# Rebuilding the opening of a gated-recurrence and two-way-maximum kernel: fp32 token halves, weights in three groups, block 0 and block 1 interleaved

## The chip, the cores and the metric

The kernel runs on one core of a Trainium2 chip, as a single launch. The metric is the device time in microseconds, the median of several runs. The engines are TensorE (PE, its weight loads listed as PEld), VectorE (DVE), ScalarE (ACT), GpSimd (POOL) and SyncE (SP), which only issues transfers.

## The reference

The inputs are `x` and `f_logit` (4 x 6144 x 256), `lower_bound` (256), and three matrices `w1`, `w2` (256 x 1024) and `w_out` (1024 x 256), all in float32.

```python
sig = 1 / (1 + exp(-f_logit))
f = lower_bound + (1 - lower_bound) * sig
for t in range(S):                       # h starts at 0 for each of the 4 sequences
    h = f[:, t] * h + (1 - f[:, t]) * x[:, t]
    y[:, t] = h
out = maximum(y @ w1, y @ w2) @ w_out    # on the 24576 rows of y
```

## The kernel before, in words

**Algebra.** With u = sigmoid(-f_logit) the input gate is (1 - lower_bound) * u, and the decay is 1 - (1 - lower_bound) * u. The kernel's recurrence is driven by v = u * x, so its y is smaller than the reference's by the factor `om` = 1 - lower_bound for each channel; the weights are multiplied by `om` instead. `nom` = lower_bound - 1 makes the decay out of u. The maximum is written as y @ w1 + relu(y @ (w2 - w1)), so the kernel needs `wd` = om * (w2 - w1) for its first layer, `w_out` as it is (`wob`, in bfloat16), and `w13` = om * (w1 @ w_out) for the part that passes by the relu.

**Tiles.** The 24576 tokens are 48 blocks of 512. Channels lie on the partitions (two halves of 128, `h` or `kc`), tokens along the free axis. The 1024 hidden units are eight groups of 128 (`fc`). The blocks are fetched in chunks: chunks 0 to 3 are one block each, the later ones two. For chunks 1 to 3, POOL's queue casts the tokens to bfloat16 on the way into SBUF (`fn`, `xn`) and PE turns them (`turn_steps`, `turn`, tiles `tT` in a PSUM pool of two). For the later chunks POOL's queue writes a bfloat16 copy to scratch memory (`scr`), and SP's queue brings it back transposed (`cross`, tiles `fT`, `xT`).

**One block.** `gate` is a sigmoid on ACT (u). `scan_steps` is a list of DVE steps: two decays (`ff`), one product over both halves (`v`), two scans (`y`). `first_layer(j, fc)` is two 512-column matmuls into a PSUM tile `dT` (pool of three) and a relu on ACT into `rt`. `second_layer` is, for each 128 tokens, two 256-column matmuls of y with `w13` and eight of `rt` with `wob`, into `psO` (pool of three); DVE copies two of them at a time to `osb`, and SP stores the block.

**Order.** The order of work on each engine is written out by hand (`tc.manual_schedule()`); only the semaphores and the slots of the pools are assigned by the framework. In the steady loop, iteration j has, for each fc, the first layer of block j, an eighth of the second layer of block j - 1, and one step of block j + 1's recurrence.

**The opening.** SP's queue fetches `lower_bound`, then block 0 as two halves of 256 tokens for each of `f_logit` and `x` (`fetch_first`, tiles `raw`, fp32), then w2 and w1 in two groups of four fc. POOL waits for the first group of w2 (`pool_waits`), then issues `w_out`, chunks 1 to 3 and the first scratch copies. Block 0's halves are cast to bfloat16 (`first_bf16`; DVE for the first half, ACT for the second), turned on PE (`first_turn`) and run through `first_recurrence` (sigmoid on ACT, decays, product and scans on DVE). `make_wd` subtracts in fp32 on DVE and scales, on ACT for group 0 and on DVE for group 1. w1 is turned on PE (`turn_w1`), copied by DVE (`keep_w1T`), and `make_w13` multiplies it with `wob`. After that block 1 is turned, and block 0's second layer follows as a whole:

```python
make_w13()
turn(turn_steps(1))
recurrence(1)
ahead("cross", cross, 4)
for fc in range(FC):
    second_layer(0, fc)
turn(turn_steps(2))
gate(2)
for fc in range(FC):
    first_layer(1, fc)
for step in scan_steps(2):
    step()
```

Then block 3 is turned and gated, and iteration j = 2 does the whole second layer of block 1 with block 3's recurrence beside it, and then the first layer of block 2.

Of the kernel before, what the change touches and what calls it, by code (L numbers as in the profile page):

```python
# [18 lines left out]
def kernel(  # L19
# [95 lines left out]
    raws = {}  # L115

    def fetch_first(k):
        nt = TB // 2
        for s in range(2):
            raw = const.tile([P, nt // P, D], FP32, name=f"raw{k}{s}")  # L120
            nc.sync.dma_start(  # L121
                out=raw[:],
                in_=srcs[s][0, k * nt : (k + 1) * nt, :].rearrange(
                    "(p i) d -> p i d", p=P
                ),
            )
            raws[k, s] = raw

    def first_bf16(k, s, copy):
        raw = raws[k, s]  # L130
        nat = const.tile([P, raw.shape[1], D], BF16, name=f"nat{k}{s}")
        copy(out=nat[:], in_=raw[:])  # L132
        raws[k, s] = nat

    def first_turn(k):
        nt = TB // 2
        for s in range(2):
            dst = ps_t.tile([P, KC, nt // P, P], BF16, name="tT")
            for q in range(nt // P):
                for h in range(KC):  # L140
                    nc.tensor.transpose(  # L141
                        dst[:, h, q, :],
                        raws[k, s][:, q, h * P : (h + 1) * P],
                        ident[:],
                    )
            raws[k, s] = dst[:].rearrange("p k i m -> p k m i")
# [48 lines left out]
    def like(t, src):  # L195
        if len(src.shape) == 3:
            return t
        return t.rearrange("p k (m i) -> p k m i", m=P)

    def scan_steps(j):  # L200
# [17 lines left out]
        def drive():  # L218
            xT = turned[j, 1]
            nc.vector.tensor_tensor(  # L220
                out=like(v[:, :, 0:nb], xT),
                in0=like(u[:, :, 0:nb], xT),
                in1=xT,
                op=ALU.mult,
            )

        def scan(h):
# [15 lines left out]
            lambda: decay(0),  # L243
            lambda: decay(1),
            drive,
            lambda: scan(0),
# [5 lines left out]
    def first_recurrence(k):  # L252
        nt = TB // 2
        cols = slice(k * nt, (k + 1) * nt)
# [4 lines left out]
        u, ff, v, y = (*(first[t] for t in ("u", "ff", "v")), ys[0])  # L259
        fT, xT = raws[k, 0], raws[k, 1]  # L260
# [3 lines left out]
        for h in range(KC):  # L264
            nc.vector.tensor_scalar(
                out=ff[:, h, cols],
                in0=u[:, h, cols],
                scalar1=nom[:, h : h + 1],
                scalar2=1.0,
                op0=ALU.mult,  # L270
                op1=ALU.add,
            )
        nc.vector.tensor_tensor(
            out=like(v[:, :, cols], xT), in0=like(u[:, :, cols], xT), in1=xT,
            op=ALU.mult,
        )
        for h in range(KC):
            nc.vector.tensor_tensor_scan(
                out=y[:, h, cols],
                data0=ff[:, h, cols],  # L280
                data1=v[:, h, cols],
                initial=y[:, h, nt - 1 : nt] if k else 0.0,
                op0=ALU.mult,
                op1=ALU.add,
            )

    def recurrence(j):
        gate(j)
        for step in scan_steps(j):
            step()  # L290
# [6 lines left out]
    lbc = const.tile([P, KC], FP32)  # L297
    waited = const.tile([P, 1], FP32)
    warm = const.tile([P, 1], FP32)
    wob = wpool.tile([P, FC, D], BF16)  # L300
    wdf = wpool.tile([P, KC, DFF], FP32)
# [3 lines left out]
    NG = 2  # L305
    NQ = FC // NG
# [140 lines left out]
    with tc.manual_schedule():  # L447
# [8 lines left out]
        for g in range(NG):  # L456
            fetch_w(g)
# [114 lines left out]
```

## Time and profile before

| | before |
|---|---|
| Median of 9 runs | 400.65 us (400.54 to 438.31) |
| The profiled execution, device time | 400.69 us |
| The profiled execution, span | 398.9 us |
| PE busy | 388.5 us in 2792 matmuls |
| DVE busy | 249.0 us |
| ACT busy | 269.5 us |
| POOL busy | 26.4 us |

The span is the stretch from the first to the last instruction of the program; the device time contains some 1.8 us around it. Busy time does not contain waits. A matmul row has a modelled end, and matmuls overlap, so the distance from one start to the next is what counts on PE. In a row of the timeline the first number is the start in microseconds from the beginning of the span, the second the length of the row, and "x8" the number of instructions merged in it; in a row of the groups, the numbers after the bar are the busy time in microseconds, the mean of one in nanoseconds, and the idle time in front with what ended it.

### The profile page before, as it was taken

Reading aid. Unit: us, or ns where it says so; the run is one execution under the profiler, and the core shown is the slowest. Engines: PE = TensorE matmul, PEld = TensorE weight load, DVE = VectorE, ACT = ScalarE, POOL = GpSimd, SP = SyncE. Lnnn points to the kernel's source line nnn. Section 1 sums busy time; section 2 is a strip of 40 time slices with the busy share of each in tenths; the row PEclk is TensorE's granted clock in tenths of the full one; section 3 lists DMA queues with packets and bytes.
Section 4 is the critical chain, followed back from the end, with each engine's and each line's share of the span. In section 5 each row is a group of like instructions: output and inputs, shape, how many; then the busy total and the mean of one; then the engine's idle time right before and its main releaser. Section 6 shows DMA issues by size and latency. Waiting matters only on the chain.

```text
span 398.9 us, 7018 instructions
## 1 busy us (share of the span) xinstructions
PE 388.5 (97%) x2792; PEld 294.9 (74%) x2792; DVE 249.0 (62%) x359; ACT 269.5 (68%) x447; POOL 26.4 (7%) x58
## 2 busy tenths in 40 slices
PE   3999999999999999999999999999999999999996
PEld 2677777777777777777777777777777777777775
DVE  5886666567656756665676567566656765665641
ACT  3656766776676667667766766776676667667761
POOL 2400010000000000000000000000000000000000
PEclk9999999999999999999999999999999999999999
DMA  7999999898998999699699999998996996762212
GB/s 244 243 244 197 160 187 285 143 250 195 194 245 193 220 219 214 183 240 193 178 180 236 209 170 247 175 211 219 195 220 176 237 209 166 165 128 89 101 53 108
DMA packets 103377, 77.01 MB, mean 193 GB/s; under 512 B 93552, under 2 KB 94064, under 8 KB 102640
## 3 DMA queue, kind: packets, MB, share of 16 engines
q1 hardware_dynamic: 100512, 51.13, 53.8%
q0 software_dynamic: 2544, 25.17, 37.3%
q8 instruction: 22, 0.36, 0.4%
q10 hardware_dynamic: 288, 0.26, 0.2%
q14 instruction: 11, 0.09, 0.1%
HBM read 53.48 MB, written 48.23 MB: 255 GB/s over the span
## 4 chain that ended last, share of the span: by engine, by line
PE 97%; DMA 2%; SPq 1%; issue 0%; DVE 0%
PE psO L410 53%; PE dT L381 42%; DMA w1n<-in_moe_w_dram 2%; PE psO L352 1%; PE tT L180 1%; PE psO L365 0%; SPq L121 0%; SPq L448 0%; SPq L321 0%; DVE osb L419 0%
## 5 line engine op out<-in xcount | busy, mean ns | idle before, releaser
L389 ACT ACTIVATE rt<-dT 128x512 bf16<-128x512 f32 x384 | 222.0, 598 | 109.6 <-PE dT L381 109.6
L410 PE MATMUL psO<-wob,rt 128*128 128x256 bf16 x1536 | 228.5, 273 | 0.0
L381 PE MATMUL dT<-y,wd 128*128 128x512 bf16 x768 | 227.3, 382 | 0.0
L410 PEld LDWEIGHTS <-rt 128*128 128x128 bf16 x1536 | 169.9, 113 | 39.9
L430 DVE COPY osb<-psO 128x512 f32<-128x512 f32 x94 | 64.9, 691 | 71.9 <-PE psO L410 71.9
L233 DVE TENSOR_TENSOR_SCAN y<-ff,y,v 128x512 bf16<-128x512 bf16 x88 | 107.9, 1267 | 0.1
L381 PEld LDWEIGHTS <-wd 128*128 128x128 bf16 x768 | 75.2, 98 | 11.0 <-issue 2.1
L410 PE MATMUL psO<-w,y 128*128 128x256 bf16 x384 | 73.3, 273 | 0.0
L410 PEld LDWEIGHTS <-y 128*128 128x128 bf16 x384 | 43.1, 113 | 39.9
L209 DVE TENSOR_SCALAR ff<-u,nom 128x512 bf16<-128x512 bf16 x94 | 28.9, 350 | 66.7 <-ACT u L190 66.7
L190 ACT ACTIVATE u<-fT 128x1024 bf16<-128x1024 bf16 x44 | 46.2, 1049 | 0.0
L220 DVE TENSOR_TENSOR v<-u,xT 128x1024 bf16<-128x1024 bf16 x44 | 30.1, 683 | 0.0
L98 POOL DMA_DIRECT2D scr<-in_f_logit_dram x22 | 10.8, 490 | 262.1 <-DMA fT<-scr 261.4
L98 POOL DMA_DIRECT2D scr<-in_x_dram x22 | 10.8, 493 | 33.6 <-DMA xT<-scr 30.3
L233 DVE TENSOR_TENSOR_SCAN y<-ff,v 128x512 bf16<-128x512 bf16 x6 | 7.0, 1206 | 0.0
L190 ACT ACTIVATE u<-tT 128x1024 bf16<-128x1024 bf16 x3 | 3.2, 1058 | 4.3 <-PE tT L180 4.3
L141 PE MATMUL tT<-ident,nat 128*128 128x128 bf16 x16 | 2.4, 307 | 2.9 <-DVE nat L132 2.5
L352 PE MATMUL psO<-ident_f,w1n 128*128 128x128 f32 x16 | 3.1, 353 | 2.2 <-DMA w1n<-in_moe_w_dram 2.2
L352 PEld LDWEIGHTS psO<-ident_f,w1n 128*128 128x128 f32 x16 | 2.7, 215 | 2.9 <-issue 2.9
L341 ACT ACTIVATE wd<-wdf,om 128x128 bf16<-128x128 f32 (+1 forms) x6 | 2.2, 427 | 3.6 <-DVE wdf L333 3.6
L141 PEld LDWEIGHTS <-nat 128*128 128x128 bf16 x16 | 1.4, 130 | 3.9 <-DVE nat L132 3.0
L333 DVE TENSOR_TENSOR wdf<-w2n,w1n 128x512 f32<-128x512 f32 (+1 forms) x5 | 4.3, 889 | 0.0
(36 smaller groups left out, 37.5 us busy)
## 6 DMA issues: line engine op xcount, KB each, us to landing
out_dram<-osb SPq DMA_DIRECT2D x47, 512.0 KB, 4.2
scr<-in_f_logit_dram POOLq DMA_DIRECT2D x22, 512.0 KB, 6.4
scr<-in_x_dram POOLq DMA_DIRECT2D x22, 512.0 KB, 8.4
w2n<-in_moe_w_dram SPq DMA_DIRECT2D x2, 512.0 KB, 6.3
w1n<-in_moe_w_dram SPq DMA_DIRECT2D x2, 512.0 KB, 7.2
fn<-in_f_logit_dram POOLq DMA_DIRECT2D x3, 256.0 KB, 8.6
xn<-in_x_dram POOLq DMA_DIRECT2D x3, 256.0 KB, 9.3
raw<-in_f_logit_dram SPq DMA_DIRECT2D x2, 256.0 KB, 3.3
```

Of the source, the lines that this page charges most:

```text
L98: nc.gpsimd.dma_start(out=scr[0:nt, :].rearrange("(p i) d -> p (i d)", p=P), in_=src.rearrange("(p i) d -> p (i d)", p=P),)
L180: nc.tensor.transpose(dst, src, ident[:])
L190: nc.scalar.activation(out=like(u[:, :, 0:nb], fT), in_=fT, func=AF.Sigmoid, scale=-1.0)
L209: nc.vector.tensor_scalar(out=ff[:, h, 0:nb], in0=u[:, h, 0:nb], scalar1=nom[:, h : h + 1], scalar2=1.0, op0=ALU.mult, op1=ALU.add,)
L220: nc.vector.tensor_tensor(out=like(v[:, :, 0:nb], xT), in0=like(u[:, :, 0:nb], xT), in1=xT, op=ALU.mult,)
L233: nc.vector.tensor_tensor_scan(out=y[:, h, 0:nb], data0=ff[:, h, 0:nb], data1=v[:, h, 0:nb], initial=init, op0=ALU.mult, op1=ALU.add,)
L333: nc.vector.tensor_tensor(out=wdf[:, :, cols].rearrange("p kc (q m) -> p kc q m", q=n), in0=half(w2n, g)[:, :, qs], in1=half(w1n, g)[:, :, ...
L352: nc.tensor.transpose(pt[:, kc, q, :], half(w1n, g)[:, kc, 2 * r + q], ident_f[:])
L381: nc.tensor.matmul(dT[:, 0:nb], lhsT=wd[:, kc, fc * P : (fc + 1) * P], rhs=y[:, kc, 0:nb], start=(kc == 0), stop=(kc == KC - 1),)
L389: nc.scalar.activation(out=rt[:, 0:nb], in_=dT[:, 0:nb], func=AF.Relu)
L410: nc.tensor.matmul(ps[:, r, :], lhsT=left, rhs=right, start=(s == 0 and (r == 0 or j == NBLK - 1)), stop=(s == n - 1 and (r == 1 or j == N ...
L430: nc.vector.tensor_copy(out=osb[:, 2 * g : 2 * g + 2, :], in_=ps[:])
```

## The change

The edits, in the order of the program:

- `lower_bound` is fetched as two rows by ACT's queue and turned on PE, instead of by SP's queue as 256 single numbers. Nothing stands ahead of the tokens on SP's queue any more.
- Block 0's halves are turned on PE as they come, in fp32, without a cast. Its four decays run on POOL, its products and scans on DVE, half by half.
- `om` moves from the weights into the drive: `scaled_product` computes x * om * u in one DVE instruction for each half of the channels, in all 48 blocks. The steps of a recurrence are now decay, drive, scan for the first half, then the same for the second: six steps, not five.
- `make_wd` is therefore a subtraction alone, straight to bfloat16, and `w13` a plain copy.
- The weights come in three groups (units 0 to 3, 4 and 5, 6 and 7), w1 ahead of w2. `w_out` comes in the same three groups, with chunk 1's tokens behind the first of them; POOL waits for the second group of w1 before it issues them.
- 9 matmuls of a constant tile (`keep_warm`) stand between the first transposes.
- In block 0's first layer, units 0 and 1 are done by halves of the tokens, and two of eight relus run on DVE. Two of the four copies of the turned w1 run on ACT.
- Block 0's second layer takes the `rt` part first (`second_first`), with block 1's and block 2's transposes between its pieces; `w13` follows; and the y part (`second_last`) is one matmul behind each fc of block 1's first layer. Block 0's output copies (DVE) follow their closing matmuls there.
- In iteration j = 2, half of block 1's second layer stands in front of the loop, the other half in it, and block 3's recurrence goes through the loop as in later blocks.

The diff, cut to its core:

```diff
-    def fetch_first(k):
...
-    def first_bf16(k, s, copy):
...
+    def first_turn(k, s):
+        dst = ps_t.tile([P, KC, HB // P, P], FP32, name="tT")
+        for q in range(HB // P):
+            for h in range(KC):
+                nc.tensor.transpose(
+                    dst[:, h, q, :],
+                    raws[k, s][:, q, h * P : (h + 1) * P],
+                    ident_f[:],
+                )
...
+    def scaled_product(out, xT, u, h):
+        nc.vector.scalar_tensor_tensor(
+            out=like(out, xT), in0=xT, scalar=om[:, h : h + 1], in1=like(u, xT),
+            op0=ALU.mult, op1=ALU.mult,
+        )
...
         return [
             lambda: decay(0),
+            lambda: drive(0),
+            lambda: scan(0),
             lambda: decay(1),
-            drive,
-            lambda: scan(0),
+            lambda: drive(1),
             lambda: scan(1),
         ]
...
+    def first_gate(k):
...
         for h in range(KC):
-            nc.vector.tensor_scalar(
+            nc.gpsimd.tensor_scalar(
                 out=ff[:, h, cols],
...
+    GROUPS = [(0, 4), (4, 2), (6, 2)]
...
+    def make_wd(fc):
         nc.vector.tensor_tensor(
+            out=wd[:, :, fc * P : (fc + 2) * P].rearrange("p kc (q m) -> p kc q m", q=2),
+            in0=units(w2n, fc, 2),
+            in1=units(w1n, fc, 2),
             op=ALU.subtract,
         )
-        for kc in range(KC):
-            if g == 0:
-                nc.scalar.mul(wd[:, kc, cols], wdf[:, kc, cols], om[:, kc : kc + 1])
-            else:
-                nc.vector.tensor_scalar_mul(
...
     with tc.manual_schedule():
-        nc.sync.dma_start(out=lbc[:], in_=lower_bound.rearrange("(h p) -> p h", p=P))
+        nc.vector.memset(heat[:], 1.0)
+        nc.vector.memset(one[:], 1.0)
+        nc.scalar.dma_start(out=lbr[:], in_=lower_bound.rearrange("(h p) -> h p", p=P))
+        for k in range(2):
+            for s in range(2):
+                fetch_first(k, s)
+        for g in range(len(GROUPS)):
+            fetch_w(g)
...
+        keep_warm(4)
+        lbc = ps_d.tile([P, KC], FP32, name="dT")
+        nc.tensor.transpose(lbc[:], lbr[:], ident_f[0:KC, 0:KC])
...
+        keep_warm(1)
+        first_turn(0, 0)
+        first_gate(0)
+        first_turn(0, 1)
...
+        first_scan(1, 0)
+        keep_warm(2)
+        turn_w1(0)
+        turn_w1(2)
+        keep_warm(2)
+        pool_waits(w1n[1][:, 0, 0:1])
...
+        fetch_wo(0)
+        ahead("fetch", fetch, 1)
+        fetch_wo(1)
+        fetch_wo(2)
         ahead("fetch", fetch, 4)
+        make_wd(0)
+        first_scan(1, 1)
+        make_wd(2)
+        make_wd(4)
+        make_wd(6)
         for fc in range(2):
+            first_half(fc, 0)
         for fc in range(2):
+            first_half(fc, 1)
+        turn_w1(4)
+        first_layer(0, 2)
+        first_layer(0, 3)
+        keep_w1T(0, nc.vector.tensor_copy)
+        first_layer(0, 4)
+        first_layer(0, 5, relu_dve)
+        first_layer(0, 6)
+        first_layer(0, 7, relu_dve)
+        keep_w1T(2, nc.vector.tensor_copy)
+        turn_w1(6)
+        keep_w1T(4, nc.scalar.copy)
+        second_first(range(4), range(0, 1))
+        t1 = turn_steps(1)
+        turn(t1[: len(t1) // 2])
+        gate(1)
+        keep_w1T(6, nc.scalar.copy)
+        second_first(range(4), range(1, 4))
+        turn(t1[len(t1) // 2 :])
+        for step in scan_steps(1):
+            step()
+        second_first(range(4, 8))
+        t2 = turn_steps(2)
+        turn(t2[: len(t2) // 2])
+        gate(2)
         make_w13()
+        turn(t2[len(t2) // 2 :])
         ahead("cross", cross, 4)
         for fc in range(FC):
-            second_layer(0, fc)
-        turn(turn_steps(2))
-        gate(2)
-        for fc in range(FC):
             first_layer(1, fc)
+            second_last(fc)
         for step in scan_steps(2):
             step()
         steps = turn_steps(3)
         turn(steps)
-        if steps:
-            gate(3)
+        gate(3)
         for j in range(2, NBLK + 1):
...
             if j == 2:
-                early = scan_steps(j + 1)
-                for fc in range(FC):
-                    second_layer(1, fc)
-                    if fc < 4:
-                        early[fc]()
-                early[4]()
+                for slot in range(FC // 2):
+                    second_layer(1, slot)
             for fc in range(FC):
                 if j < NBLK:
                     first_layer(j, fc)
                 if j > 2:
                     second_layer(j - 1, fc)
+                else:
+                    second_layer(1, FC + fc, 2 * FC)
...
-                if fc == 0 and 2 < j < NBLK - 1:
+                if fc == 0 and j < NBLK - 1:
                     scans = scan_steps(j + 1)
```

## The prediction

> **What bounds the kernel now.** I read the page's busy times first, then the chain that ended last in order of time, then the timeline of the first 45 us, then groups by form. The page says that TensorE sets the time:
>
> ```profile
> PE 388.5 (97%) x2792; PEld 294.9 (74%) x2792; DVE 249.0 (62%) x359; ACT 269.5 (68%) x447; POOL 26.4 (7%) x58
> PE 97%; DMA 2%; SPq 1%; issue 0%; DVE 0%
> ```
>
> The change touches no matmul of the steady blocks, so it can win only where PE is not yet working at full rate. The chain in order of time shows where that is (start, length, what):
>
> ```profile
> 3.64 6.36 DMA w1n<-in_moe_w_dram
> ...
> 10.14 1.95 PE psO L352 x8
> 12.09 3.40 PE dT L381 x8
> 15.49 0.94 PE psO L352 x8
> 16.43 1.78 PE dT L381 x8
> 18.21 1.75 PE psO L365 x16
> ...
> 26.11 3.77 PE dT L381 x16
> 29.88 0.89 PE tT L180 x16
> 30.77 4.37 PE psO L410 x40
> ```
>
> Two things are to be seen. PE waits for weights until 10 us. And the same eight matmuls take 3.40 us before 15.3 us and 1.78 after, the same transposes 1.95 and 0.94: PE runs at half rate until 15.3 us, although the page's clock row shows 9 there. Still, half rate alone does not set this stage, as VectorE rows of the timeline show:
>
> ```profile
> 10.72 2.12 DVE L333 TENSOR_TENSOR wdf<-w2n,w1n 128x256 f32<-128x256 f32 x3
> ...
> 12.75 1.28 DVE L359 CAST w1T<-psO 128x512 bf16<-128x512 f32 x2
> ...
> 13.95 1.07 DVE L333 TENSOR_TENSOR wdf<-w2n,w1n 128x512 f32<-128x512 f32 x1
> ...
> 16.71 0.62 DVE L343 TENSOR_SCALAR wd<-wdf,om 128x256 bf16<-128x256 f32 x2
> ```
>
> DVE works without a pause until the last pair of first-layer weights `wd` is there, at 17.33. A faster PE would have waited for it. From there on PE is packed.
>
> **Part 1: the weights come ready earlier.** Taking `lower_bound` off SP's queue starts the token loads at 0.74 instead of 1.25, so everything behind shifts by 0.5 us. The weights are as many bytes in the same queue, behind the same 1 MB of tokens; the second half megabyte landed at 10.0 (chain: 3.64 + 6.36) and now lands at about 9.5. The two together hold w1 and w2 of units 0 to 3, as before. DVE then runs: one subtraction straight to bf16 (128x512: 1.08, the L333 row of that size), the last half scan (0.7, L278), three more subtractions (1.06 each): 9.5 + 1.1 + 0.6 + 3.2 = 14.4. The six scaling steps on ACT and four on DVE are gone from this chain because `1 - lower_bound` now sits in the drive. Last `wd`: 14.4 against 17.33, 2.9 us earlier.
>
> The pieces before it fit. Casts fall away; token transposes in fp32 cost 4 x 0.213 (L352 at half rate) instead of 4 x 0.107, on an idle PE. The four decays on Pool: a 128x128 select took 0.29, a 128x1 copy 0.18, so 0.8 ns per element and some 0.4 us for 256; bounds 0.28 (DVE's own L265 row) and 1.2 (three times the estimate). The scans that wait for them start only at 6.6, behind the drives; up to 1.0 us each costs nothing, 1.2 costs 0.6 us. The nine 512-column warming matmuls (0.43 each at half rate) run where PE waits for data; the last two may delay the first layer by 0.3 if PE is still slow.
>
> Pool's wait moves from w2 (8.67) to the second w1 group (about 10.2), and w_out, cut in three, and the loads of blocks 1 to 3 are queued behind it. The transfers are bound by bandwidth then: POOL's waits for `fn` and `xn` end at 17.05 and 18.37, so half a megabyte is read in 1.3 us, and the order counts, not the issue. The last weights were issued at 4.68 and took 8.0 (median of the two 7.2, the first 6.36), so they now end at 12.2, and w_out's first half at 13.5. It is first needed at 16.3; two microseconds more are covered.
>
> **Part 2: block 0 to block 2, on PE.** At 14.4 two units of layer 1 remain (4 x 0.216), then four transposes (0.48): 15.8. The next PSUM slot needs ACT's copy of transposed w1, behind a relu: 16.3. Then without a pause: 32 second-layer matmuls (0.109 each, from 4.37 / 40), 32 bf16 transposes (0.056), w13 (1.75), 16 matmuls of block 1 (0.216), 8 closing ones (0.109): 3.5 + 1.8 + 1.75 + 3.45 + 0.9 = 11.4, ending at 27.7. The same work, with block 2 turned, ended at 29.7 before (the timeline's next transposes start at 29.71). Gain so far: 2.0 us. That DVE's drives are now two per block matters little up to here.
>
> **Part 3: it is given back before block 2.** In the changed order block 0's last output copy stands ahead of block 2's recurrence on DVE, and it waits for the closing matmul, which is now the last one after block 1's first layer. So block 2's recurrence can start only at 28.0:
>
> ```profile
> L233 DVE TENSOR_TENSOR_SCAN y<-ff,y,v 128x512 bf16<-128x512 bf16 x8 | 9.9, 1271 | 0.1
> L220 DVE TENSOR_TENSOR v<-u,tT 128x1024 bf16<-128x1024 bf16 x3 | 3.6, 1215 | 0.0
> L430 DVE COPY osb<-psO 128x512 f32<-128x512 f32 x5 | 3.3, 682 | 0.5 <-PE psO L410 0.5
> ```
>
> Copy 0.62 (start to start), two decays 0.61, two drives at 0.68, two scans 2.46: y of block 2 is whole at 33.05. PE has only block 3's transposes (0.9) and half of block 1's second layer (20 x 0.109 = 2.2) to put in between. It also waits some 1.3 us inside the transposes, because the built program puts both turned tiles of block 3 into one PSUM bank, and the second waits for ACT's sigmoid of the first; that wait lies within DVE's chain and adds nothing. PE resumes at 33.1 with 15 x 0.216 + 20 x 0.109 = 5.4 to go: block 3 starts at 38.5. Before:
>
> ```profile
> 34.97 4.32 PE L381 MATMUL dT<-y,wd 128*128 128x512 bf16 x18
> ```
>
> The 17th of these is block 3's first; it starts 0.59 before the end at 39.29, at 38.7. Of 2.0 us, 0.2 is left.
>
> **Part 4: the steady blocks.** PE's work is the same. Per block one 0.68 drive (1024 wide) becomes two of 512 with a scalar. No row shows this instruction: 0.42 if it keeps the old rate (half of 683 plus the start), 1.27 if it runs like the scan. I take 0.68, the 1215 row for half the width, its nearest in PSUM. In the timeline, block 4's scans end at 45.87 and its first matmuls with that y run at 46.5 to 46.7; the new order (decay, drive, scan, copy, decay, drive, scan, from 41.09) ends at 41.09 + 0.61 + 2 x 0.66 + 2.45 + 0.66 = 46.1. About 0.6 us of slack remain, so up to 1.0 us per drive costs nothing.
>
> **Sum.** The profiled execution took 400.69 for a span of 398.9, against a median of 400.65. 400.65 - 0.2 = 400.4 (0.2%, or 0.8 us, is about what a measurement of this kernel can tell from no change).
>
> **The clock.** The sum needs full rate by about 12 us. In the trace full rate came at 15.3: 5.2 us after PE became busy with transposes (10.14), 3.4 us after the matmuls began (11.88). If any activity counts, the changed kernel, busy from 1.2 us on with small gaps, is fast by about 6.4, and the sum stands. If matmuls alone count, they run without a break only from 10.1, and four transposes at 12.7 break them: full rate between 13.5 and 17.
>
> The Trainium skill, TensorE: Matmul & The Clock Gate, Part 1, gives about 3.4 us of sustained activity for this switch, and Part 4 says that transposes do not count as busy in the same way. That speaks against this opening, and would put the time near 402; this trace agrees with the 3.4 us but cannot tell the two readings apart.
>
> **Rivals.** (B) The clock rises late, the slower side. Each microsecond at half rate past 12 costs PE half a microsecond, as it is packed: 13.5 gives 401.1, 15.3 gives 402, 17 gives 402.9. For it: 3.4 us fits the start of the matmuls exactly. Against it: PE is hardly idle from 1.2 us on, and nothing in the trace says that transposes leave the clock down. It decides from about 13.5 on.
>
> (C) The gain is larger. If weights land 0.5 us earlier still (no 4-byte packets of `lower_bound` in the queue ahead), PE follows one for one until its own work binds, at most 0.7: 399.7. For it: the first token load took 2.8 us from issue (1.25) to the cast that waits for it (4.05).
>
> (D) The new drive takes 1.1 us: two of them are 0.84 longer than assumed, 0.24 beyond the slack, times 44 blocks: DVE sets the time, 411. Against it: no arithmetic row but the scan is that slow.
>
> **How the numbers follow.** Forecast 0.42 (399.9 to 401.0), B 0.36, C 0.18, D 0.04. Range 399.4 to 402.6: it leaves out D and the ends of B and C. Faster: C and a little of the forecast, 0.20. Same: most of the forecast and B's early end, 0.42. Slower: 0.38.
>
> **What would show it.** Right: last `wd` near 14.4; an idle PE of about 1 us in front of block 2's first layer, released by DVE's scan; block 3 starting within 0.3 of 38.5. B shows as first-layer matmuls 0.43 apart past 13 us. Wrong altogether: PE packed through 28 to 33 us (a gain of 2 us), or PE waiting for y in the steady blocks.

## The result, and the profile after

| | before | after |
|---|---|---|
| Median | 400.80 us (34 runs) | 402.28 us (11 runs, 401.57 to 403.60) |
| Ratio to before, 95% interval | 1 | 1.0034 [1.0026, 1.0042] |
| The profiled execution, device time / span | 400.69 / 398.9 us | 402.40 / 400.5 us |
| PE / DVE busy | 388.5 / 249.0 us | 389.5 / 283.1 us |

The change makes the kernel slower by 0.34%, 1.4 us. The forecast was no change (400.4); the time lies inside the range. In some executions TensorE's clock falls back to half for stretches long after the opening; the ratios leave these out, while the medians and the profiles of a few experiments below contain them.

The page's busy line and its shares of the chain, after:

```profile
PE 389.5 (97%) x2798; PEld 295.8 (74%) x2798; DVE 283.1 (71%) x399; ACT 267.3 (67%) x438; POOL 29.8 (7%) x64
...
PE 93%; DMA 4%; DVE 1%; POOL 1%; SPq 1%; issue 0%
```

PE still carries the time, but it held 97% of the chain before and 93% now: DMA has 4% instead of 2%, and POOL and DVE have 1% each. The chain in order of time (start, length, what) shows where:

```profile
3.59 7.82 DMA w1n<-in_moe_w_dram
11.41 0.05 issue
11.46 0.43 POOL waited L335
11.89 0.67 POOL wob L327
12.56 0.54 POOL fn L105
13.11 0.53 POOL xn L105
13.64 0.49 POOL wob L327
14.13 6.43 DMA wob<-in_moe_w_out_dram
20.55 0.04 issue
20.60 1.69 PE psO L427 x14
...
29.29 0.69 DVE osb L452
29.98 0.26 DVE ff L212
30.24 0.67 DVE v L194
30.93 1.28 DVE y L231
...
34.50 0.38 PE dT L386
```

Two stretches are new. Up to 20.6 us the chain runs over the second group of w1, POOL's wait for it, POOL's issues, and the last piece of `w_out`: block 0's second layer waits for that piece. From 29.3 to 34.5 it runs over DVE: block 0's last output copy, then block 2's recurrence, as the prediction's Part 3 had it.

Where the microseconds are, by the steps of the prediction (starts from the timeline, before where it had the same step):

| step | before | predicted | after |
|---|---|---|---|
| second half megabyte of weights landed | 10.00 | 9.5 | 10.69 |
| block 0's first layer starts, on the first `wd` | 11.88 | 10.6 | 11.90 |
| last piece of `wd` ready | 17.33 | 14.4 | 14.70 |
| all of `w_out` landed | 15.52 | not priced | 20.55 |
| block 0's second layer starts | | 16.3 | 17.08 |
| block 3's transposes start | | 27.7 | 29.09 |
| block 2's y whole, PE resumes | | 33.1 | 34.50 |
| block 3's first layer starts | 38.70 | 38.5 | 39.91 |
| from there to the last matmul's start | 356.16 | 356.16 | 356.16 |
| from there to the end of the span | 4.05 | 4.05 | 4.47 |

The last three rows add up to the span, and the middle one of them is the same to 0.01 us: the steady blocks did not change. So the loss in the span, 1.62, is 1.21 ahead of block 3 and 0.42 behind the last matmul. Against the forecast it is 1.41 and 0.42, which added to 400.4 make 402.2.

### The profile page after: what moved, and what is told of

It reads as the page before. It is cut to its first block, busy times and chain, and to the rows that moved or that the text cites. A ratio compares the mean times of both kernels' runs of the same rounds, so it can differ in the third digit from the quotient of the medians.

```text
span 400.5 us, 7081 instructions
## 1 busy us (share of the span) xinstructions
PE 389.5 (97%) x2798; PEld 295.8 (74%) x2798; DVE 283.1 (71%) x399; ACT 267.3 (67%) x438; POOL 29.8 (7%) x64
## 4 chain that ended last, share of the span: by engine, by line
PE 93%; DMA 4%; DVE 1%; POOL 1%; SPq 1%; issue 0%
PE psO L474 51%; PE dT L386 40%; DMA w1n<-in_moe_w_dram 2%; DMA wob<-in_moe_w_out_dram 2%; DVE y L231 1%; PE psO L364 0%; PE psO L427 0%; SPq L120 0%; DVE v L194 0%; POOL wob L327 0%; SPq L320 0%; PE tT L171 0%; PE psO L443 0%; DVE osb L452 0%; POOL fn L105 0%
## 5 line engine op out<-in xcount | busy, mean ns | idle before, releaser
L474 PEld LDWEIGHTS <-rt 128*128 128x128 bf16 x1504 | 166.5, 113 | 41.2
L231 DVE TENSOR_TENSOR_SCAN y<-ff,y,v 128x512 bf16<-128x512 bf16 x88 | 113.0, 1284 | 3.1
L494 DVE COPY osb<-psO 128x512 f32<-128x512 f32 x92 | 62.5, 679 | 33.4 <-PE psO L474 33.4
L212 DVE TENSOR_SCALAR ff<-u,nom 128x512 bf16<-128x512 bf16 x94 | 32.8, 349 | 62.2 <-ACT u L181 62.2
L474 PE MATMUL psO<-w,y 128*128 128x256 bf16 x376 | 71.8, 273 | 0.0
L194 DVE SCALAR_TENSOR_TENSOR v<-xT,om,u 128x512 bf16<-128x512 bf16 x88 | 65.6, 746 | 0.0
L98 POOL DMA_DIRECT2D scr<-in_f_logit_dram x22 | 10.8, 489 | 260.6 <-DMA fT<-scr 260.0
L194 DVE SCALAR_TENSOR_TENSOR v<-tT,om,u 128x512 bf16<-128x512 bf16 (+1 forms) x10 | 6.2, 635 | 2.2 <-ACT u L259 1.8
L527 PE MATMUL dT<-heat 128*128 128x512 bf16 x9 | 3.7, 515 | 1.5 <-DVE one L513 1.5
L338 DVE TENSOR_TENSOR wd<-w2n,w1n 128x512 bf16<-128x512 f32 x4 | 3.3, 878 | 1.6 <-DMA w2n<-in_moe_w_dram 1.6
L452 DVE COPY osb<-psO 128x512 f32<-128x512 f32 x2 | 1.4, 690 | 4.3 <-PE psO L443 4.3
```

Source lines behind the costliest of these rows:

```text
L98: nc.gpsimd.dma_start(out=scr[0:nt, :].rearrange("(p i) d -> p (i d)", p=P), in_=src.rearrange("(p i) d -> p (i d)", p=P),)
L194: nc.vector.scalar_tensor_tensor(out=like(out, xT), in0=xT, scalar=om[:, h : h + 1], in1=like(u, xT), op0=ALU.mult, op1=ALU.mult,)
L212: nc.vector.tensor_scalar(out=ff[:, h, 0:nb], in0=u[:, h, 0:nb], scalar1=nom[:, h : h + 1], scalar2=1.0, op0=ALU.mult, op1=ALU.add,)
L231: nc.vector.tensor_tensor_scan(out=y[:, h, 0:nb], data0=ff[:, h, 0:nb], data1=v[:, h, 0:nb], initial=init, op0=ALU.mult, op1=ALU.add,)
L338: nc.vector.tensor_tensor(out=wd[:, :, fc * P : (fc + 2) * P].rearrange("p kc (q m) -> p kc q m", q=2), in0=units(w2n, fc, 2), in1=units(w ...
L474: nc.tensor.matmul(ps[:, r, :], lhsT=left, rhs=right, start=(s == 0 and (r == 0 or j == NBLK - 1)), stop=(s == n - 1 and (r == 1 or j == N ...
```

## The experiments

All runs stand beside runs of the kernel before on the same chip. "Landing" is that of the second half megabyte of weights, "block 3" the start of its first layer, "tail" the stretch from the last matmul's start to the end of the span; with 356.16 between them, the last two make the span.

| kernel | landing | all of `w_out` | block 3 | tail | median | ratio to before |
|---|---|---|---|---|---|---|
| before | 10.00 | 15.52 | 38.70 | 4.05 | 400.80 | 1 |
| after | 10.69 | 20.55 | 39.91 | 4.47 | 402.28 | 1.0034 [1.0026, 1.0042] |
| e2 POOL issues earlier | 10.63 | 18.55 | 39.21 | 4.47 | 401.43 | 1.0005 [0.9995, 1.0015] |
| e3 e2, weights in two groups | 10.27 | 17.83 | 39.08 | 3.52 | 400.56 | 0.9983 [0.9974, 0.9992] |
| e4 no warming matmuls | 10.48 | 20.39 | 40.27 | 4.50 | 402.61 | 1.0025 [1.0012, 1.0038] |
| e6 e3, recurrence early | 10.73 | 19.25 | 37.46 | 3.53 | 398.94 | 0.9952 [0.9939, 0.9964] |
| e7 decays on DVE | 10.34 | 20.56 | 39.92 | 4.46 | 402.29 | 1.0029 [1.0017, 1.0041] |
| e8 w2 ahead of w1 | 10.80 | 21.61 | 40.97 | 4.47 | 403.65 | 1.0060 [1.0046, 1.0074] |
| e11 a second load of `lower_bound` | 9.44 | 18.72 | 39.34 | 4.31 | 401.33 | 1.0010 [1.0001, 1.0020] |
| e13 six tiny loads | 10.46 | 19.69 | 39.06 | 3.65 | 401.64 | 1.0011 [1.0000, 1.0022] |
| e14 e13, POOL and recurrence early | 10.70 | 18.44 | 37.15 | 3.64 | 398.78 | 0.9939 [0.9923, 0.9955] |
| b1 before, early matmuls | 10.07 | 15.67 | 38.76 | 3.96 | 401.97 | 1.0005 [0.9991, 1.0019] |
| b3 before, decays on POOL | 10.29 | 15.27 | 39.11 | 4.17 | 401.38 | 1.0002 [0.9990, 1.0014] |

### POOL's wait (e2)

```diff
-        pool_waits(w1n[1][:, 0, 0:1])
+        pool_waits(w1n[0][:, 0, 0:1])
```

> The changed kernel with POOL waiting for the first group of w1 (landed at 9.3) instead of the second (11.4). Theory A (w_out and the tokens of block 1 come late because POOL issues late): POOL issues 2 us earlier, the hole in the transfers between 12.3 and 13.5 us closes, w_out's second half lands by 19 instead of 20.6, PE's waits before 20.6 go: 0.5 to 0.7 us faster, about 401.7. Theory B (the same bytes share one bandwidth): the weights land later by what w_out lands earlier, and the time stays within 0.3 us or gets worse.

Ratio 1.0005 against 1.0034: 1.2 us by the ratios, 0.85 by the medians, and 0.70 in block 3's start. POOL's first issue moved from 11.84 to 9.47 and all of `w_out` was there at 18.55. What the queue did in between is read best in the windows of 12 to 13 and 13 to 14 us (length, busy times of the engines, clock, DMA share, GB/s), first of the changed kernel, then of the kernel before, then of this run:

```profile
12.00:13.00 1.00, 1.00 (x10) 0.82 (x9) 1.00 (x2) 0.14 (x1) 1.00 (x2) 1.00 0.30 96
13.00:14.00 1.00, 0.98 (x8) 0.55 (x7) 1.00 (x2) 0.95 (x2) 1.00 (x3) 1.00 0.38 67
```

```profile
12.00:13.00 1.00, 1.00 (x4) 0.35 (x3) 1.00 (x2) 0.76 (x4) 1.00 (x3) 1.00 1.08 205
13.00:14.00 1.00, 1.00 (x3) 0.21 (x2) 1.00 (x3) 1.00 (x3) 0.36 (x1) 1.00 1.11 207
```

```profile
12.00:13.00 1.00, 1.00 (x10) 0.83 (x9) 1.00 (x2) 0.19 (x1) 1.00 (x3) 1.00 1.16 263
13.00:14.00 1.00, 0.97 (x7) 0.55 (x7) 1.00 (x3) 0.90 (x2) 0.91 (x2) 1.00 1.08 196
```

In the changed kernel the DMA engines are two thirds idle for two microseconds: the weights are nearly through and POOL's loads, issued only from 11.84 on, have not begun to move. The weights themselves were not held up by the earlier issue (10.63 against 10.69). The chain of this run has no transfer of `w_out` in it:

```profile
3.08 7.55 DMA w2n<-in_moe_w_dram
...
10.73 1.07 DVE wd L338
...
19.83 1.75 PE psO L427 x16
```

### The recurrence of block 2 (e1, e5, and e6 against e3)

```diff
+        for step in scan_steps(2):
+            step()
         for fc in range(FC):
             first_layer(1, fc)
             second_last(fc)
-        for step in scan_steps(2):
-            step()
```

> The changed kernel with one edit: block 2's recurrence stands ahead of block 1's first layer on DVE, so it no longer queues behind block 0's last output copy. Theory 1 (the gain is given back in that queue): the two idle stretches of PE before block 2 (1.2 us inside block 3's transposes, 0.6 us at the first matmul of block 2) vanish and the time falls by 2.0 us, to about 400.3. Theory 2 (only late data costs, PE would be idle elsewhere): the idle time moves and the time stays within 0.5 us of 402.3.

> The changed kernel with block 2's recurrence written ahead of the loop over block 1's first layer and block 0's closing matmuls, nothing else. Theory (what layer 2 inside block 0 gained is given back because block 2's recurrence waits on DVE behind block 0's last output copy, and block 3's two turned tiles share a PSUM bank): y of block 2 is whole before block 1's first layer ends, the gaps of 1.4 and 1.0 us on TensorE are gone, about 400.3 us, 2.0 below the changed kernel. Rival (DVE is full there anyway): the copies of block 0's output or of w1T come later in their place, TensorE waits for them, and the time stays within 0.5 us of 402.3.

Neither gave a usable time: e1's six executions took 407 to 836 us, e5's 401.85 to 454. In e5's profile, whose clock was at full rate from 4.41 to 76 us, block 3 started at 37.69 instead of 39.91, with both waits gone; the theory's 2.0 was 2.2. The comparison that gives a time is e6, which is e3 with this edit and nothing else:

> Three edits of the changed kernel together: block 2's recurrence is written ahead of block 1's first layer, Pool issues w_out's fetches after the first weight transfer instead of the third, and the weights come as two halves instead of a half and two quarters. Theory (the three losses lie in series: late w_out, the later weights, and the recurrence of block 2 that queues behind block 0's output copies): the gains add, 0.85 and 0.87 as the runs with Pool's edit and with both showed, and about 2.0 for the recurrence, so some 398.6 against 402.3 of the changed kernel, ratio to the kernel before about 0.995. Rival (the earlier recurrence only moves the wait: DVE is then late with block 0's output copies or w1T copies): 400.3 to 400.8, as without it.

It took 398.94, ratio 0.9952 against 0.9983 of e3: 1.2 us by the ratios, 1.6 by the medians, and block 3 starts 1.62 earlier, although the clock of its profiled execution was back at half from 9.59 to 13.00 us. (e14, below, has the same program as e2 up to block 3 but for this edit; there it is 2.06, 37.15 against 39.21.) The two waits in the timeline of the changed kernel,

```profile
30.86 0.61 PE L171 MATMUL tT<-ident,xn 128*128 128x128 bf16 x8 [1.16 <-ACT u L181]
...
34.50 0.38 PE L386 MATMUL dT<-y,wd 128*128 128x512 bf16 x1 [0.63 <-DVE y L231]
```

have become packed PE work in the chain of e6:

```profile
28.91 0.89 PE tT L171 x16
29.81 2.18 PE psO L474 x20
31.99 0.05 issue
32.04 0.38 PE dT L386
```

The three edits together beat both kernels, the one before by 0.48% [0.36, 0.61].

### Two groups, and the end of the run (e3, e13, e14)

e3 is e2 with the weights and `w_out` in two groups of four units:

```diff
-    GROUPS = [(0, 4), (4, 2), (6, 2)]
+    GROUPS = [(0, 4), (4, 4)]
...
-        fetch_wo(2)
```

> As the run before (POOL waits for the first group of w1), with the weights and w_out in two groups of four units again instead of a half and two quarters, so rows of 2 KB throughout. If the smaller pieces slow the queue, the weights of the first group land earlier than 10.7 and the last before 13.0, and the time falls by 0.3 to 0.8 us against that run; if the size of the pieces does not matter, the first group lands as it did, the second subtraction waits longer for its data, and the time is the same or up to 0.5 us longer.

It gained 0.87 us over e2 on the same chip, but block 3 started only 0.13 earlier. The gain is in the tail: 3.52 instead of 4.47. The trace shows why the tail has steps. After its last store SP runs nine closing waits, in an order of semaphores that is the same in the changed kernel, e3 and e13; where nothing is left to wait for, one follows the other after 0.06 to 0.07 us. The stores take eight semaphores in turn. Which of the nine waits the last store ends depends on how many transfers the program has issued:

| kernel | the last store ends closing wait | behind that wait | tail |
|---|---|---|---|
| after | 3 of 9, at 398.81 | six waits until 399.23, SP's next instruction at 399.58 | 4.47 |
| before | 9 of 9, at 397.60 | SP's next instructions at 397.68 and 398.03 | 4.05 |
| e3 | 9 of 9, at 397.86 | SP's next instruction at 397.94 | 3.52 |

The waits are not all of it. Of the 0.95 between the changed kernel and e3, the stretch up to the last store's landing makes 0.12, the six waits behind it 0.40, and the stretch from the ninth wait to the end of the span 0.43 (1.33 against 0.90), for which the trace names no cause.

e3 has two loads fewer on SP's queue, which moves the last store back by two of eight semaphores. Six more should do the same:

```diff
+            if j == 20:
+                for q in range(6):
+                    nc.sync.dma_start(out=spare[:, q : q + 1], in_=lower_bound.rearrange("(a p) -> a p", a=1)[:, q : q + 1])
```

> The changed kernel with six loads of one number each on SP's queue in the middle of the run, which nobody reads. The eight semaphores of such transfers go round in order, so the last store moves from the second of SP's nine closing waits to the last. Theory (the order of the closing waits costs the end of the run): the stretch from the last matmul's start to the end of the span falls from 4.47 to some 3.5 to 4.1 us, and the time by 0.4 to 0.9 us to 401.4 to 401.9. Rival (the stretch is set by the stores' landing alone): it stays at 4.4 to 4.5 and the time at 402.0 to 402.6.

> The changed kernel with block 2's recurrence early, Pool's early issue and the six tiny loads, but the weights in three groups. Theory (two groups brought only another place for the last store in the closing waits): 398.7 to 399.2, as with two groups (398.94). Rival (two groups speed the opening by themselves): 399.6 to 400.0.

The wait that the last store ends moved to the ninth in both, and the tails fell to 3.65 and 3.64. (The expectation called it the second wait; it was the third.) e13 took 401.64, 0.64 below the changed kernel (0.9 by the ratios), and its profile shows that both parts went together: the waits behind the last store are gone, and the stretch from the ninth wait to the end is 0.92. In its profiled execution `w_out` also came 0.86 earlier without any edit there, so its block 3 start is not to be read as an effect. e14 with three groups took 398.78, like e6 with two: the two groups bring the tail and hardly anything else. Why the kernel before, with the last store at the ninth wait too, still has 1.31 behind that wait and a tail of 4.05 stays open; its stretch from 397.68 to 398.03 is not named by the trace.

### What makes the weights late (e7, e8, b2, b3, b4, e9, e11)

In the eleven kernels that have the changed kernel's loads (the change, e1 to e8, e13, e14) the second half megabyte landed at 10.1 to 10.8, 7.1 to 7.7 us after its issue at 3.08. In the kernel before and in b1, b3 and b4, with the issue at 3.65, it took 6.36 to 6.64. The largest difference lies in the window of 5 to 7 us, changed kernel first, then the kernel before:

```profile
5.00:7.00 2.00, 1.55 (x12) 1.11 (x11) 1.39 (x3) 0.93 (x2) 0.94 (x2) 1.00 0.82 183
```

```profile
5.00:7.00 2.00, 1.04 (x9) 0.64 (x8) 1.50 (x4) 1.53 (x3) 0.00 (x0) 1.00 1.04 339
```

POOL is the one engine busy in the first and not in the second (the fifth busy time, 0.94 and 0). Hence e7 (`nc.gpsimd.tensor_scalar` to `nc.vector.tensor_scalar` in `first_gate`) and its mirror b3 (block 0's decays on POOL in the kernel before, with POOL's wait and loads behind them):

> The changed kernel with block 0's four decays on DVE as before, so that Pool computes nothing between 1.3 us and its wait for the weights. The stretch from 5 to 7 us moves 178 and 188 GB/s in the changed kernel, 399 and 279 in the one before. Theory (Pool's decays, at 5.7 to 6.6 and 7.3 to 8.5, slow the transfers): those two stretches rise above 300 GB/s, the second half megabyte of weights lands at 9.3 to 9.8 instead of 10.7, and the time falls by 0.6 to 1.0 us to about 401.4. Rival (the transfers are slow for another reason): it lands at 10.4 to 10.8 and the time stays within 0.4 us of 402.3, since four decays on DVE of some 0.2 us each fit into its wait for the weights.

> One part of the change alone: the kernel before with block 0's decays on Pool, and Pool's wait for the weights and its loads of w_out behind them in program order. Theory (Pool's decays slow the transfers): the stretches at 6 to 9 us fall from 279, 338 and 408 GB/s to some 200 to 250, the second half megabyte of weights lands at 10.6 to 11.0 instead of 10.0, and the time rises by 0.5 to 1 us to 401.3 to 401.8. Rival (they don't): it lands at 9.9 to 10.1, and the time is within 0.4 us of the kernel before, as the four decays of some 0.5 us lie beside DVE's drive products.

Each moved the landing by 0.3 us in the direction of the theory, a fraction of the difference and no more than kernels with equal openings differ by; the times did not move (402.29 against 402.28; ratio 1.0002 for b3). POOL's decays cost nothing that these runs can tell. The order of the loads:

```diff
-        for w, src in ((w1n, moe_w1), (w2n, moe_w2)):
+        for w, src in ((w2n, moe_w2), (w1n, moe_w1)):
```

> The changed kernel with the two weights of each group fetched in the order of the kernel before, w2 ahead of w1. Theory (the order decides how the transfers run between 5 and 7 us, since it is the one difference that all kernels with slow stretches there share with each other on SP's queue and not with the kernel before): the second half megabyte lands at 9.3 to 9.8 and the time falls by 0.6 to 1.0 us. Rival (the order is nothing): it lands at 10.4 to 10.8, the time is within 0.3 us of 402.3, and w1's turns on TensorE start some 1.4 us later in the shadow of that wait.

The order was nothing for the landing (10.80), but the time rose to 403.65, which no theory expected. PE's timeline in this run: the turns of w1, which stand ahead of the first layer on PE, now begin at 10.84 instead of 9.34 and take 1.98 us instead of 1.23, as the clock is back at half from 10.55 to 13.96. The first layer begins at 13.47 although its `wd` was ready at 11.99.

The fp32 turns alone (b4) and the load of `lower_bound` by ACT in the kernel before (b2):

```diff
-        nc.sync.dma_start(out=lbc[:], in_=lower_bound.rearrange("(h p) -> p h", p=P))
+        nc.scalar.dma_start(out=lbc[:], in_=lower_bound.rearrange("(h p) -> p h", p=P))
```

> One part of the change alone: the kernel before with its first 512 tokens turned by TensorE as fp32, without the four casts to bf16 on DVE and ACT. Theory (the fp32 turns slow the transfers): the second half megabyte lands at 10.6 to 11.0 instead of 10.0, and what DVE saves, two casts of some 0.3 us, is lost again, so the time is 401 to 401.5. Rival (they don't): it lands at 9.9 to 10.3, the last piece of wd comes 0.3 to 0.7 us earlier than 17.33 as DVE's queue is shorter, and the time falls by 0.2 to 0.6 us.

> The kernel before with the lower bound's load issued by ACT instead of SP, so that all loads on SP's queue are issued 0.5 us earlier and nothing else changes. As the prediction had it (arrival follows issue): the second half megabyte of weights lands near 9.5 instead of 10.0 and the time falls by 0.3 to 0.5 us. Rival (arrival does not follow issue by half a microsecond, because the transfers themselves run slower between 4 and 7.5 us wherever they start): it lands at 9.9 to 10.7, and the time is within 0.3 us of the kernel before or above it.

b4 took 401.44, ratio 1.0001 [0.9992, 1.0011], landing 10.24: no part in it, and DVE's saved casts brought nothing in time. b2 gave ratio 0.9993 [0.9976, 1.0010], but its weights landed at 9.24, as early as the prediction had them. So an issue 0.5 us earlier does bring an earlier landing, where ACT loads the 256 numbers one by one; the changed kernel loads them as two rows. That is the next edit: e9 takes b2's load into the changed kernel, e10 into e6, e12 repeats e10, and e11 keeps the row load and adds the column load, which nobody reads:

```diff
+        nc.scalar.dma_start(out=lbx[:], in_=lower_bound.rearrange("(h p) -> p h", p=P))
         nc.scalar.dma_start(out=lbr[:], in_=lower_bound.rearrange("(h p) -> h p", p=P))
```

> The changed kernel with the lower bound loaded straight into its columns by ACT, as in the variant of the kernel before whose weights came at 9.24, in place of two rows that TensorE turns. Theory (the row load and what hangs on it delays the weights): the second half megabyte lands at 9.2 to 9.8 instead of 10.1 to 10.8, and the time falls by 0.6 to 1.0 us. Rival (the lower bound's load has no part in it): it lands at 10.1 to 10.8, and the time is 402.0 to 402.8, as block 0's first drive still waits for its tokens until about 5.5 us.

> The three edits together (recurrence of block 2 early, Pool's early issue of w_out, weights as two halves), and the lower bound loaded by ACT straight into its columns. Theory (the lower bound's row load delays the weights): 398.0 to 398.4. Rival (no part in it): 398.7 to 399.2, as with the three edits alone (398.94).

> The changed kernel with its row load of the lower bound, and ahead of it on ACT the column load as well, whose result nobody reads. Theory (the row load slows the transfers): the second half megabyte of weights lands at 10.1 to 10.8 as in the changed kernel, and the time is 402.0 to 402.8. Rival (the column load's small packets, which hold up the first tokens until about 4.3 us, are what spares the weights the slow stretch between 5 and 7 us): it lands at 9.2 to 9.7, and the time is 401.4 to 401.9.

> The three edits and the column load by ACT once more. If the column load brings what it brought to the changed kernel alone (0.5 us): 398.1 to 398.6, below the 398.94 of the three edits without it; if that was chance: 398.8 to 399.2. Its trace should show the second half megabyte at 9.2 to 9.5 and no wait of TensorE over 0.3 us between 20 us and the end of the opening.

With the column load the landing is 9.33 (e9), 9.38 (e10), 9.44 (e11) and 9.43 (e12), 6.2 to 6.4 us after the issue. The kernel before and b1 to b4 have this load too, on SP's queue or ACT's, and took 6.2 to 6.6. The window of e11 is full again:

```profile
5.00:7.00 2.00, 2.00 (x9) 1.63 (x9) 0.22 (x2) 0.59 (x1) 0.00 (x0) 1.00 1.05 397
```

The row load does not slow the transfers, since it is in e11 too. Adding 256 packets of four bytes makes the weights come 1.2 us sooner, and the tokens later (the first quarter lands at 4.2 instead of 3.4). How, the runs do not show; from 3 to 4 us e11 moves 90 GB/s and the changed kernel 299, as if a slow stretch came early instead of late. The ratios: e9 1.0017 [1.0007, 1.0028], e11 1.0010, e10 0.9936 [0.9921, 0.9951], and e12, which is the same program, 0.9917 [0.9896, 0.9937]; these last two rest on three and two executions, so e6 and e14 stay the better founded ones.

In e11 the earlier weights did not bring an earlier `wd`, as its chain shows:

```profile
1.24 3.38 DMA lbr<-in_lower_bound_dram
...
5.52 1.72 PE tT L132 x8
...
10.37 0.52 issue
10.89 1.04 DVE wd L339
...
11.98 1.15 PE dT L405 x8
```

The first subtraction starts at 10.89 with its weights there since 9.44: the row load, issued behind the column load, is there only at 4.62, PE's turn of it stands ahead of block 0's, and so block 0's recurrence is still on DVE. What e11 gained came through POOL, whose first issue moved from 11.84 to 10.37 and `w_out` from 20.55 to 18.72, as in e2. In e9, which has no row load, the earlier weights did bring an earlier `wd`, and the first layer starts 0.95 earlier than in the changed kernel:

```profile
9.87 1.03 DVE L338 TENSOR_TENSOR wd<-w2n,w1n 128x512 bf16<-128x512 f32 x1
```

```profile
10.95 1.17 PE L404 MATMUL dT<-y,wd 128*128 128x256 bf16 x8 [0.65 <-DVE wd L338]
```

(The clock of e9's profiled execution was at 0.85 from 7.83 us on, so its later rows on PE are not compared.)

### The clock (e4, b1)

e4 leaves out the nine `keep_warm` matmuls; b1 gives the kernel before five of them in place of its eight early transposes and two pairs later.

> The changed kernel without its nine warming matmuls. If transposes count as activity for TensorE's clock, full rate comes some 3.4 to 5 us after the first transpose, by 9 us, and the time stays within 0.2 us. If only matmuls count, full rate comes 3.4 us after the first layer begins, near 15 us, and the time grows by 0.8 us (PE bound), to about 403.1.

> The kernel before with five matmuls on a constant tile in place of its eight early transposes, and two more pairs of them around the first turns of the weights: TensorE is at full rate from about 5 us instead of 15.3, nothing else changes. As the prediction had it (DVE, busy until the last piece of wd at 17.33, sets the stage, not TensorE's rate): the last piece of wd stays at 17.0 to 17.4 and the time within 0.4 us of the kernel before. Rival (the half rate costs the stage): the eight first-layer matmuls and the transposes at full rate bring 1 to 1.6 us.

In e4 full rate came at 14.92, 3.2 us after the first first-layer matmul at 11.69; fp32 transposes had run since 3.3 us. In the changed kernel it came at 5.03, 3.6 us after the first warming matmul (1.46); PE worked without a longer pause in between. That distance is no constant: in e2, e3, e5 to e8, e13 and e14, whose warming matmuls start at 1.46 too, full rate came at 4.41 to 7.79. The late clock cost e4 0.36 us in block 3's start, and its ratio, 1.0025, cannot be told from 1.0034.

That e4's transposes left the clock low does not show that transposes do not count. They had pauses: from 4.68 to 8.09 and from 8.09 to 11.51, two stretches of 3.41 us (the time for which the clock fell back in e6 and in e8), PE was busy for 2.53 and 2.25. In e13 they were denser, and full rate came at 7.64, in the middle of them:

```profile
3.48 0.61 PE L528 MATMUL dT<-heat 128*128 128x512 bf16 x1
3.88 2.98 PE L132 MATMUL tT<-ident_f,raw 128*128 128x128 f32 x12
7.06 0.90 PE L132 MATMUL tT<-ident_f,raw 128*128 128x128 f32 x4 [0.20 <-DMA raw<-in_x_dram]
```

The 3.41 us ahead of that rise hold fp32 transposes alone, 3.21 us of them; in e11 it is the same (3.28, rise at 9.12). Ordinary matmuls had run before in both, so whether transposes would do it without any is not shown. b1 did not do what it was made for: its five matmuls end at 3.8, PE pauses for 0.95, and the clock rose only at 14.62; its unchanged time (1.0005) says nothing on half rate. In b4, however, the clock happened to rise at 13.75 and the timeline then shows PE waiting for DVE:

```profile
16.75 0.61 DVE L343 TENSOR_SCALAR wd<-wdf,om 128x256 bf16<-128x256 f32 x2
...
17.16 1.08 PE L381 MATMUL dT<-y,wd 128*128 128x512 bf16 x4 [0.43 <-DVE wd L343]
```

That is the prediction's claim on the kernel before: a faster PE waits for the last pair of `wd`.

## Why the prediction was wrong

**Part 1 is the step that failed, twice.** First, "the transfers are bound by bandwidth then [...] and the order counts, not the issue" and "two microseconds more are covered". POOL's move behind the second group of w1 was priced only against `w_out`'s first piece (13.5 predicted, 15.69 measured, no wait). What POOL loads behind that piece was not priced at all: block 1's `xn` landed at 19.29, `w_out`'s second piece at 19.90 and its last, which PE needed at 20.17 (two matmuls of 0.109 behind 19.95), at 20.55. The transfers were not bound by bandwidth: POOL was released at 11.41, not 10.2, its first issue ended at 12.6, and the first of its loads landed 3.9 us after its issue, so the DMA engines were two thirds idle for 2 us. The three late landings cost PE 0.07, 0.16 and 0.43 us, 0.66 together:

```profile
19.34 0.62 PE L171 MATMUL tT<-ident,xn 128*128 128x128 bf16 x8
19.95 0.38 PE L427 MATMUL psO<-wob,rt 128*128 128x256 bf16 x2
20.60 1.69 PE L427 MATMUL psO<-wob,rt 128*128 128x256 bf16 x14 [0.27 <-DMA wob<-in_moe_w_out_dram]
```

In e2, which moves only the release, the same transposes and matmuls follow each other without a pause, and block 3 starts 0.70 earlier.

Second, "now lands at about 9.5". It landed at 10.69, and the first `wd` came 1.2 us later than forecast. The forecast followed the last `wd` alone, which was only 0.3 late because the three later subtractions came every 0.6 to 0.8 us (2.28 for three) instead of 1.06. But PE is released by the first: from 11.90 to 16.6 it is packed with the first layer and the turns, and waits then only for ACT's copy of w1. So the second layer starts 0.8 late. That the landing set the first `wd` is seen on DVE, which stood idle ahead of it (its row, 1.63 us, ended by the DMA of w2), and in e9. Why the weights came late is known only so far: without the packets of the column load they took 1.2 us longer from issue to landing (e11), where the prediction let everything arrive as much earlier as it was issued.

On PE these add up: 0.78 at 17.08 and 0.66 up to 20.60 are the 1.4 at block 3. They are not two causes side by side, though. The second group of w1 landed 1.2 later than forecast as well, and it releases POOL; in e11, where it landed at 10.19, PE waits for none of POOL's loads. And as long as those are late, earlier weights alone gain nothing: in e7 the landing and the first layer came 0.35 earlier, so that the second layer started at 16.74 instead of 17.08, but the last piece of `w_out` landed at 20.56, PE went on at 20.60 as in the changed kernel, and block 3 started at 39.92.

```profile
16.74 0.60 PE L427 MATMUL psO<-wob,rt 128*128 128x256 bf16 x4 [0.20 <-ACT w1T L358]
...
20.60 1.69 PE L427 MATMUL psO<-wob,rt 128*128 128x256 bf16 x14 [0.26 <-DMA wob<-in_moe_w_out_dram]
```

**Part 2 and Part 3 were right in size.** From the second layer's start to block 3's transposes 11.4 was predicted and 12.0 measured, the 0.66 of POOL's loads included. From there to block 3 10.8 was predicted and 10.82 measured, with both waits where they were foretold: PE idle ahead of block 2's first layer, released by DVE's scan. e6 and e14 show that this give-back is DVE's order alone, since moving block 2's recurrence took it away.

**Part 4 held.** The new drive adds 0.67 us to DVE's chain behind the decay's end, where 0.68 was assumed; its group, with the mean length of a row, 746 ns:

```profile
L194 DVE SCALAR_TENSOR_TENSOR v<-xT,om,u 128x512 bf16<-128x512 bf16 x88 | 65.6, 746 | 0.0
```

DVE is 34 us busier, and the steady blocks together are not a hundredth of a microsecond longer. POOL's decays took 0.47 to 0.68 each, within the bounds given (0.28 to 1.2).

**The tail was in no rival.** 0.42 us is a quarter of the loss; the number of transfers was never weighed as a cost.

**The rivals.** B (late clock) did not happen: full rate at 5.03, and for a rise at 14.92, as in e4, the prediction's rule (half a microsecond for each past 12) gives 1.5. On PE that is nearly right: from the first layer's start to the second layer's e4 took 6.40 us, the changed kernel 5.18. But 0.66 of these 1.22 fall where the changed kernel waits for POOL's loads and e4 does not, and e4's first layer began 0.21 earlier, so only 0.36 reach block 3. C had its sign wrong: without the four-byte packets the weights come later. D did not happen. The loss had the size of B's lower half for another reason.

**The clock rule.** The Trainium skill, TensorE: Matmul & The Clock Gate, gives 3.4 us of sustained activity in Part 1. The 3.41 us for which the clock fell back in e6 and e8 agree; from the first warming or first-layer matmul to the rise it was 3.2 us in e4 and 3.6 in the changed kernel, but 2.95 to 6.33 in the others of this opening. Its Part 4 says that transposes do not count as busy the same way. The prediction reckoned this against the change; e13 and e11, where the clock rose behind 3.41 us of nothing but fp32 transposes, go against it, and the measurement decides here: of the prediction's two readings, the one in which any dense activity counts fits these traces.

## What to carry to other kernels

When a wait that releases a queue is moved, price every transfer behind it at the point where its last byte is needed, not only the first; an idle window in the DMA rows of the profile shows such a hole at once. When a stage is sped up, find the next instruction that the saved time would have to pass, here a recurrence behind an output copy on DVE: moving that one step brought 1.2 us, where the rebuilt opening without it lost 1.4. And split the span at a repeated stretch that did not change: what lies ahead of it and behind it then adds up to the hundredth of a microsecond.

## What the hardware showed unexpectedly

- 256 packets of four bytes, read by nobody, at 2.6 to 4.3 us made half a megabyte of weights land 1.2 us earlier (9.44 against 10.69) and the kernel 0.24% faster by the ratios (1.0010 against 1.0034). The Trainium skill, DMA: Bandwidth & Descriptors, Rules for kernel authors, advises against a last dimension that is not contiguous, since it becomes one descriptor for each element. For the tokens beside it the runs agree (the first quarter 0.8 us later); for the program as a whole the measurement says the opposite here.
- Transposes with hardly a pause went with the rise of the clock as matmuls did: in e13 and e11 the 3.41 us ahead of it hold 3.21 and 3.28 us of fp32 transposes and no other matmul.
- The end of the program, from the last matmul's start on, took 3.52 to 4.47 us. Six loads that nobody reads, issued in the middle of the run, took 0.82 off it (e13); the closing waits behind the last store's are 0.40 of that, the rest the trace does not name.
